# An mLSTM cell feeding a GELU MLP: the first chunk's order on TensorE, and split matmuls in the fifth chunk

## The chip, the cores and the metric

The kernel runs on one core of a Trainium2 chip. The metric is the device time of one execution in microseconds (us). Each time shown is that of one run; the median of the runs stands for the kernel. A profiled execution, with a trace of every instruction, comes beside them.

## The reference, cut to what matters

The first block is an mLSTM cell over 4 batches, 8 heads, 768 steps and a head size of 40; the second is a two-layer MLP on its output, laid out as 3072 tokens of 320 features.

```python
for t in range(S):                                   # S = 768
    m_new = np.maximum(f_gate[:, :, t] + m, i_gate[:, :, t])
    f_stab = np.exp(f_gate[:, :, t] + m - m_new)
    i_stab = np.exp(i_gate[:, :, t] - m_new)
    C = f_stab * C + i_stab * einsum('bhd,bhe->bhde', v_t, k_t)
    n = f_stab * n + i_stab * k_t
    h_tilde = einsum('bhde,bhe->bhd', C, q_t)
    denom = np.maximum(np.abs(einsum('bhd,bhd->bh', n, q_t)), 1.0)
    y[:, :, t] = sigmoid(o_gate[:, :, t]) * h_tilde / denom
x = y.transpose(0, 2, 1, 3).reshape(3072, 320)
h = x @ w_in                                         # 320 x 2048
g = h * sigmoid(1.702 * h)
out = g @ w_out                                      # 2048 x 320
```

All inputs and the output are float32.

## The kernel before, in words

Time is cut into six chunks of 128 steps, `w` = 0 to 5. Within a chunk the cell is computed like attention: scores of keys and queries, multiplied by exponents of gates, times values; a state is carried from chunk to chunk. Each chunk then gives 512 tokens (4 batches of 128) to the MLP: `up` or `up_fast` over 8 pairs `j` of 128 hidden features, then `down` or `down_fast`. Chunks 1 to 5 use Strassen-like forms (`up_fast`, `down_fast`), and the attention of chunk `w + 1` is threaded between the blocks of `down` of chunk `w`. There is no scheduler: every engine executes its instructions in the order in which the Python code issues them, and waits on semaphores where data or a buffer is not ready.

The first chunk, before any MLP work exists, stands alone at the start (lines 767 to 788). For each batch `b` it runs `transposes(0, b)` (keys and queries through TensorE into p_t, L347, copied by ScalarE), `scores(0, b - 1)` (p_s, L397, and on VectorE the multiplication L399 into `wt`), `weights(0, b)` (bf16 matmuls into p_w, L372 to L378, and exponents on ScalarE, L380). After the loop come `columns(0)` (L325, L327, L328), then for each batch `open_first` (a tanh of the output gate on ScalarE, L765) and `values` (L440, 8 matmuls with 41 moving columns each, two records per matmul in the trace; then `outputs` on VectorE, L418 to L427, and a copy on POOL, L431). Batch 0's values stand in the last turn of the loop, ahead of `scores(0, 3)`. Then four `seam` calls turn y into the MLP's layout: three TensorE transposes into p_x (L480) and a ScalarE copy into xT (L482). `up(0, j)` (L557, L563) needs all four.

`keep_busy(n, bank)` issues n bf16 matmuls of a tile of zeros; their results are not read. In the kernel before, the last seam has one ahead of its transposes and two behind, into the second bank of p_x.

MLP weights arrive as 512-column pieces of raw 32-bit words and are changed in place by `convert(n)`: two ScalarE operations (L229, L230), then four on VectorE (L231 to L236). Pieces 0 and 1 are converted within the first loop; piece 2 (`w_in_x`, the 64-row rest of w_in, read at L563) between the last two seams; the others during the up- and down-projections of chunk 0 (`weights_in`).

All DMAs of the start are issued by SyncE in one order: gates, keys and queries per batch with pieces 0 and 1 between, then v and o gates per batch, then pieces 2 to 9.

PSUM has two pools: `ps_a` (p_t, p_w, p_cols, p_x and others; a ring of two tiles of two banks) and `ps_m` (p_s, p_o, p_h, p_out; a ring of four tiles of one bank).

In `up_fast`, `rest()` (L629 to L632) multiplies the last 64 of the 320 features: two matmuls of 64 rows each, 512 columns, in the upper and lower half of the array, for the rows `row0` and `row1`. For even `j` it ends the accumulation, for odd `j` it begins it, so that two calls stand next to each other.

Of the kernel before, what the change touches and what calls it, by code (L numbers as in the profile page):

```python
# [8 lines left out]
FP = mybir.dt.float32  # L9
U32 = mybir.dt.uint32  # L10
# [7 lines left out]
L = 128  # L18
# [8 lines left out]
def kernel(  # L27
# [13 lines left out]
    B, H, S, D = q.shape  # L41
# [3 lines left out]
    NW = S // L  # L45
# [4 lines left out]
    W = B * L  # L50
# [16 lines left out]
    ps_m = ctx.enter_context(tc.tile_pool(name="ps_m", bufs=4, space=PSUM))  # L67
    ctx.enter_context(tc.manual_schedule())

    V, A, G, T = nc.vector, nc.scalar, nc.gpsimd, nc.tensor  # L70
# [15 lines left out]
    w_in_x = const.tile([128, NF // 2, 128], FP, name="w_in_x")  # L86
# [62 lines left out]
    pieces = []  # L149
# [4 lines left out]
    bits = {}  # L154
# [31 lines left out]
    def keep_busy(n, bank):  # L186
        for _ in range(n):
            T.matmul(bank, idle, idle.unsqueeze(1).to_broadcast([128, 4, 128]), start=True, stop=True)

    p_idle = ps_m.tile([128, W], FP, tag="m", name="p_idle")  # L190
# [31 lines left out]
    kT, qT, ys, xT, gs, o_ps, sums, vw, x_row = {}, {}, {}, {}, {}, {}, {}, {}, {}  # L222


    def convert(n):

        lo, hi, dst = bits[n][:, :, 0], bits[n][:, :, 1], pieces[n][0]
        dst_u = dst.bitcast(U32)
        A.activation(out=dst, in_=hi.bitcast(FP), func=AF.Abs)  # L229
        A.activation(out=lo, in_=lo, func=AF.Copy, scale=2.0 ** -29)  # L230
        V.tensor_scalar(out=dst, in0=dst, scalar1=HI_MIN, scalar2=HI_MAX, op0=OP.max, op1=OP.min)  # L231
        V.tensor_scalar(out=dst_u, in0=dst_u, scalar1=3, scalar2=0x3FFFFFFF, op0=OP.logical_shift_left,
                        op1=OP.bitwise_and)
        V.scalar_tensor_tensor(out=dst_u, in0=hi, scalar=0xC0000000, in1=dst_u, op0=OP.bitwise_and,
                               op1=OP.bitwise_or)
        V.tensor_tensor(out=dst_u, in0=dst_u, in1=lo, op=OP.add)  # L236
# [59 lines left out]
    def slot(i, x):  # L296

        return slice((x ^ i) * HL, (x ^ i) * HL + HL)

    def banks(name):  # L300
        return ps_a.tile([128, 2, 512], FP, tag="a", name=name)
# [131 lines left out]
    def values(w, c):  # L433
        if w == 0:
            hs = slice(c * H, (c + 1) * H)
            po = ps_m.tile([L, H, D1], FP, tag="m", name="p_o")
            for p in range(NP):
                for i in range(2):
                    h = 2 * p + i
                    T.matmul(po[:, h, :], wt[w, c][:, p, i, :], v_st[:, c * H + h, :], start=True, stop=True)  # L440
            outputs(w, hs, po)
            return
        hs = slice(c * PH, (c + 1) * PH)
        po, pi = banks("p_o"), banks("p_i")

        for j in range(NJ):
            for i in range(2):
                for x in range(2):
                    t, r = slice(x * HL, x * HL + HL), slot(i, x)
                    T.matmul(po[t, i, j * D1:(j + 1) * D1], wt[w, c][r, j, i, :], v_st[r, c * PH + 2 * j + i, :],  # L450
                             start=True, stop=True)
        for j in range(NJ):
            b, p = 2 * c + j // NP, j % NP
            for i in range(2):
                r = slice(i * 64, i * 64 + D)
                for x, s in enumerate((state[w % 2], state_mid)):
                    t = slice(x * HL, x * HL + HL)
                    T.matmul(pi[t, i, j * D1:(j + 1) * D1], qT[w, b][r, p, t], s[r, c * NJ + j, :], start=True,  # L458
                             stop=True)
        u = work.tile([L, PH, D1], FP, tag="u", name="u")  # L460
        v = u.rearrange("s (j i) d -> s i j d", i=2)
        g = cols[w][:, BH + c * PH:BH + (c + 1) * PH].rearrange("s (j i) -> s i j", i=2).unsqueeze(3)
        view = lambda z: z[:, :, 0:NJ * D1].rearrange("s i (j d) -> s i j d", d=D1)
        V.tensor_tensor(out=v, in0=view(pi), in1=g.to_broadcast([L, 2, NJ, D1]), op=OP.mult)
        V.tensor_tensor(out=v, in0=view(po), in1=v, op=OP.add)
        outputs(w, hs, u)
# [3 lines left out]
            xT[w] = work.tile([128, 3, B, L], FP, tag="xT", bufs=1, name="xT")  # L470
        return xT[w]

    def seam(w, c, b, busy=0, after=0):
        both = banks("p_x")
        px = both[:, 0, 0:3 * L]
        keep_busy(busy, both[:, 1, :])
        y = ys[w, c][:, b, :]
        for x in range(3):
            y_x = y[:, 256:384] if x == 2 else y[:, x:256:2]
            T.transpose(px[:, x * L:(x + 1) * L], y_x, ident)  # L480
        keep_busy(after, both[:, 1, :])
        A.copy(out=x_of(w)[:, :, 2 * c + b, :], in_=px.rearrange("r (x t) -> r x t", t=L))  # L482

    def x_square(c, n):
# [125 lines left out]
    def up_fast(w, j):  # L610

        x, rest_x = temps[w], xT[w].rearrange("p c b t -> p c (b t)")
        late = j % 2 == 0
        p1, row0 = (ps_m.tile([128, W], FP, tag="m", name="p_h") for _ in range(2))
        both = banks("p_h")
        row1 = both[:, 0, :]
        flat = both.rearrange("p i t -> p (i t)")  # L620
        left, right = slice(0, half_w), slice(half_w, W)
        f = lambda c, i: w_in_sb[:, c, (2 * j + i) * 128:(2 * j + i + 1) * 128]

        def product(n, out, start, stop):
            a = {1: lambda: f(0, 0), 2: lambda: f(1, 0), 3: lambda: s_in[:, 2, j], 4: lambda: f(1, 1),
                 5: lambda: s_in[:, 0, j], 6: lambda: s_in[:, 1, j], 7: lambda: f(0, 1)}[n]()
            T.matmul(out, a, x[n], start=start, stop=stop)  # L627

        def rest():  # L629
            for i, row in enumerate((row0, row1)):  # L630
                r = slice(i * 64, i * 64 + 64)
                T.matmul(row, w_in_x[r, j, :], rest_x[r, 2, :], start=not late, stop=late)  # L632

        def row_0():
            product(2, row0[:, left], late, False)
            product(3, row0[:, right], False, not late)

        def row_1():
            product(4, row1[:, left], late, False)
            product(7, row1[:, right], False, not late)  # L640

        if not late:
            rest()
        product(1, p1[:, left], True, True)
        if late:
            row_0()
        product(5, both[:, 1, left], True, True)
        product(6, both[:, 1, right], True, True)
        row_1()
        if late:  # L650
            rest()
        else:
            row_0()
        y = work.tile([L, 2, DM + 64], FP, tag="y", name="parts").rearrange("p a b -> p (a b)")
        u2 = second[w]
        g = gs[w, j] = gp.tile([128, 2, W], FP, tag="g", name="g")
        A.copy(out=y[:, left], in_=p1[:, left])  # L657
        if j:
            gelu_fast(w, j - 1)
        V.tensor_tensor(out=u2, in0=both[:, 1, right], in1=y[:, left], op=OP.add)  # L660
        V.tensor_tensor(out=y[:, half_w:3 * half_w].rearrange("p (a t) -> p a t", a=2),  # L661
                        in0=flat[:, half_w:3 * half_w].rearrange("p (a t) -> p a t", a=2),
                        in1=u2.unsqueeze(1).to_broadcast([128, 2, half_w]), op=OP.add)
        V.tensor_tensor(out=g[:, 1, :], in0=row1, in1=y[:, half_w:3 * half_w], op=OP.add)  # L664
        u = y.rearrange("p (a t) -> p a t", t=half_w)[:, 0:3:2]
        g0 = g[:, 0, :].rearrange("p (a t) -> p a t", a=2)
        if j < NF // 2 - 2:
            A.copy(out=g[:, 0, :], in_=row0)  # L668
            G.tensor_tensor(out=g0, in0=g0, in1=u, op=OP.add)  # L669
        else:  # L670
            V.tensor_tensor(out=g0, in0=row0.rearrange("p (a t) -> p a t", a=2), in1=u, op=OP.add)
# [91 lines left out]
    def open_first(b):  # L763
        hs = slice(b * H, (b + 1) * H)
        A.activation(out=eo[0][:, hs, :], in_=eo[0][:, hs, :], func=AF.Tanh, scale=0.5)  # L765

    for b in range(B + 1):
        if b < B:
            transposes(0, b)
        if b == B:  # L770
            open_first(0)
            values(0, 0)
        if b:
            scores(0, b - 1)
        if b in (1, 2):
            convert(b - 1)
        if b < B:
            weights(0, b)
    load_gates(1)
    load(1, "kq")  # L780
    columns(0)
    for b in range(1, B):
        open_first(b)
        values(0, b)
    for b, (busy, after) in enumerate(((0, 0), (0, 0), (0, 0), (1, 2))):
        seam(0, b // 2, b % 2, busy, after)
        if b == 2:
            convert(2)

    beside = [((3, 4), (10, 11, 12, 13, 14)), ((5, 6, 7), (15,)), ((8, 9, 10), (16,)), ((11, 12, 13), (17, 18, 19)),  # L790
              ((14,), ()), ((15,), ()), ((16,), ()), ((17,), ()), ((18,), ()), ((19,), ())]
# [112 lines left out]
```

## Time and profile before

| what | us |
|---|---|
| median of 3 runs | 479.73 |
| the runs | 479.73, 481.18, 478.07 |
| the profiled execution | 478.76 |
| its span, first to last instruction | 477.1 |

| engine | busy us | share of the span |
|---|---|---|
| PE (matmul) | 470.1 | 99% |
| PEld (weight load, overlaps PE) | 379.2 | 79% |
| DVE | 341.0 | 71% |
| ACT | 189.4 | 40% |
| POOL | 157.8 | 33% |

In the profile's lines "PE L440 MATMUL p_o<-v_st,wt" is TensorE, line 440 of the kernel, the output's tile and the tiles read. The page cuts the span into 40 slices of 11.9 us; its row PEclk gives the TensorE clock granted, in tenths. In a timeline a line has the start, the duration, the engine, the line, the operation, shapes and count, and in brackets the idle time before it and who ended it. In the chain of waits a line has the start, the time spent, and on what.

### The profile page before, as it was taken

What the parts mean: (1) busy time and instruction counts of PE and PEld (TensorE: products, weight loads), DVE (VectorE), ACT (ScalarE), POOL (GpSimd) and SP (SyncE); (2) the same over time, 40 slices, a digit from 0 to 9 for tenths busy, and PEclk for the clock granted to TensorE, in tenths of its full rate; (3) what the DMA queues carried; (4) which work ended last, traced back from release to release, by engine and by line L of the source; (5) the groups of instructions that cost most, each with busy time, mean ns of one, the idle gap of its engine ahead of it and who ended that gap; (6) DMA issues with size and microseconds to landing.
All of it is one profiled execution on the core that took longest, in us unless ns stands there. A gap on an engine that the chain in (4) does not pass through costs nothing.

```text
span 477.1 us, 12024 instructions
## 1 busy us (share of the span) xinstructions
PE 470.1 (99%) x4884; PEld 379.2 (79%) x4884; DVE 341.0 (71%) x701; ACT 189.4 (40%) x429; POOL 157.8 (33%) x145
## 2 busy tenths in 40 slices
PE   8999999999999999999999999999999999999997
PEld 5874446777767999767999877999877999876997
DVE  6755977989968877868877868887867866644612
ACT  4646567900434810354820254720254720164200
POOL 6020002500299720157620157620157620047100
PEclk9969999999999999999999999999999999999999
DMA  7999988005999105999205899305899205100000
GB/s 178 177 319 171 261 119 210 4 3 137 207 169 138 20 18 136 164 184 139 33 18 136 157 184 136 44 19 136 150 173 147 48 19 127 37 0 1 0 30 27
DMA packets 157591, 52.18 MB, mean 109 GB/s; under 512 B 127296, under 2 KB 154976, under 8 KB 157536
## 3 DMA queue, kind: packets, MB, share of 16 engines
q1 hardware_dynamic: 149536, 49.78, 56.4%
q10 hardware_dynamic: 8000, 1.64, 1.7%
q8 instruction: 38, 0.62, 0.6%
q14 instruction: 17, 0.14, 0.1%
HBM read 43.86 MB, written 7.54 MB: 108 GB/s over the span
## 4 chain that ended last, share of the span: by engine, by line
PE 95%; DVE 2%; DMA 1%; issue 1%; ACT 1%; SPq 0%; DVEq 0%
PE p_out L732 32%; PE p_h L627 26%; PE p_h L632 8%; PE p_out L678 7%; PE p_h L557 6%; PE p_c L535 3%; PE p_o L450 2%; PE p_o L440 2%; PE p_s L408 2%; PE p_i L458 2%; PE p_h L563 2%; PE p_t L347 1%; PE p_s L397 1%; DMA q_sq<-in_q_dram 1%; PE p_x L480 0%
## 5 line engine op out<-in xcount | busy, mean ns | idle before, releaser
L669 POOL TENSOR_TENSOR g<-g,parts 128x512 f32<-128x512 f32 x30 | 38.2, 1274 | 190.3 <-DVE parts L661 183.0
L657 ACT COPY parts<-p_h 128x256 f32<-128x256 f32 x40 | 15.0, 374 | 151.8 <-PE p_h L627 123.5
L732 PE MATMUL p_out<-w_out_sb,g 128*128 128x160 f32 x480 | 69.6, 301 | 0.2 <-ACT g L608 0.2
L732 PEld LDWEIGHTS p_out<-w_out_sb,g 128*128 128x128 f32 x480 | 66.5, 190 | 1.3 <-ACT g L608 0.5
L627 PE MATMUL p_h<-xT,w_in_sb 128*128 128x256 f32 x240 | 66.9, 388 | 0.0
L608 ACT ACTIVATE g<-g 128x512 f32<-128x512 f32 x80 | 50.1, 631 | 40.4 <-DVE g L664 25.8
L627 PEld LDWEIGHTS p_h<-xT,w_in_sb 128*128 128x128 f32 x240 | 43.7, 190 | 20.2 <-issue 7.6
L737 DVE TENSOR_TENSOR o_sb<-o_sb,p_out 128x160 f32<-128x160 f32 x70 | 21.5, 318 | 41.4 <-PE p_out L732 40.8
L732 PE MATMUL p_out<-t_sb,s 128*128 128x160 f32 x320 | 47.1, 300 | 0.0
L660 DVE TENSOR_TENSOR t_x<-p_h,parts 128x256 f32<-128x256 f32 x40 | 16.8, 421 | 39.3 <-PE p_h L632 34.9
L732 PEld LDWEIGHTS p_out<-t_sb,s 128*128 128x128 f32 x320 | 44.4, 190 | 0.2
L627 PE MATMUL p_h<-t_x,s_in 128*128 128x256 f32 x160 | 41.1, 379 | 0.0
L632 PE MATMUL p_h<-xT,w_in_x 64*128 64x512 f32 x160 | 39.7, 615 | 0.0
L384 ACT ACTIVATE wt<-wt,cols 128x64 f32<-128x64 f32 x160 | 38.8, 333 | 0.1
L525 POOL TENSOR_TENSOR vw<-v_st,cols 128x656 f32<-128x656 f32 x12 | 16.5, 1393 | 61.5 <-ACT cols L331 61.5
L678 PE MATMUL p_out<-w_out_sb,g 128*128 128x320 f32 x128 | 36.0, 436 | 0.7 <-DVE w_out_sb L236 0.7
L627 PEld LDWEIGHTS p_h<-t_x,s_in 128*128 128x128 f32 x160 | 30.3, 190 | 4.2
L678 PEld LDWEIGHTS p_out<-w_out_sb,g 128*128 128x128 f32 x128 | 23.8, 190 | 10.6 <-DVE w_out_sb L236 1.2
L557 PE MATMUL p_h<-xT,w_in_sb 128*128 128x512 f32 x64 | 29.5, 604 | 0.8 <-ACT xT L482 0.8
L661 DVE TENSOR_TENSOR parts<-p_h,t_x 128x512 f32<-128x512 f32 x40 | 27.7, 692 | 3.5
L668 ACT COPY g<-p_h 128x512 f32<-128x512 f32 x30 | 17.4, 581 | 29.3 <-PE p_h L632 24.4
L664 DVE TENSOR_TENSOR g<-p_h,parts 128x512 f32<-128x512 f32 x40 | 27.7, 692 | 1.4
(186 smaller groups left out, 839.0 us busy)
## 6 DMA issues: line engine op xcount, KB each, us to landing
wt<-m_row SPq DMA_DIRECT2D x40, 128.0 KB, 3.9
k_sq<-in_k_dram SPq DMA_DIRECT2D x16, 320.0 KB, 6.1
q_sq<-in_q_dram SPq DMA_DIRECT2D x16, 320.0 KB, 10.0
out_dram<-o_sb SPq DMA_DIRECT2D x24, 160.0 KB, 2.3
eo<-in_o_gate_dram SPq DMA_DIRECT2D x5, 640.0 KB, 9.1
bits<-in_moe_w_in_dram SPq DMA_DIRECT2D x6, 512.0 KB, 8.2
q_sq<-x_row SPq DMA_DIRECT2D x10, 256.0 KB, 2.9
v_st<-in_v_dram SPq DMA_DIRECT2D x14, 160.0 KB, 5.1
```

Source lines behind the costliest of these rows:

```text
L384: A.activation(out=x[:, h, :], in_=x[:, h, :], func=AF.Exp, scale=-1.0, bias=cols[w][:, c * PH + h:c * PH + h + 1])
L557: T.matmul(ph[j][i], w_in_sb[:, c, f * 128:(f + 1) * 128], x[:, c, :], start=(first and c == 0), stop=(not first and c == 1))
L608: A.activation(out=gs[w, j][:, i, :], in_=gs[w, j][:, i, :], func=AF.Gelu_apprx_sigmoid)
L627: T.matmul(out, a, x[n], start=start, stop=stop)
L632: T.matmul(row, w_in_x[r, j, :], rest_x[r, 2, :], start=not late, stop=late)
L661: V.tensor_tensor(out=y[:, half_w:3 * half_w].rearrange("p (a t) -> p a t", a=2), in0=flat[:, half_w:3 * half_w].rearrange("p (a t) -> p a ...
L664: V.tensor_tensor(out=g[:, 1, :], in0=row1, in1=y[:, half_w:3 * half_w], op=OP.add)
L668: A.copy(out=g[:, 0, :], in_=row0)
L669: G.tensor_tensor(out=g0, in0=g0, in1=u, op=OP.add)
L678: T.matmul(po, gs[w, f // 2][:, f % 2, b * L:(b + 1) * L], w_out_sb[:, f, :], start=(f == 0), stop=(f == NF - 1))
L732: T.matmul(po, a(f), b[:, f, :], start=(f == 0), stop=(f == NH - 1))
L737: V.tensor_tensor(out=dst, in0=x, in1=po, op=OP.add)
```

## The change

It has three parts.

In the first chunk, `values(0, 0)` moves ahead of `weights(0, 3)`, and `values(0, 1)` ahead of `scores(0, 3)`, each with its `open_first`; the other two stand between the seams. `convert(2)` is parted: its ScalarE half stands after seam 0, its VectorE half after the last seam.

`keep_busy` now writes to a tile of its own, `spare`, from the ring `ps_m`, and nine of its matmuls stand behind the seams (2, 2, 3, 2) in place of three.

In `up_fast`, at `w == NW - 2` (the fifth chunk) alone, `rest()` issues its matmuls in halves of 256 columns.

```diff
     def convert(n):
-
-        lo, hi, dst = bits[n][:, :, 0], bits[n][:, :, 1], pieces[n][0]
-        dst_u = dst.bitcast(U32)
+        convert_begin(n)
+        convert_end(n)
+
+    def convert_begin(n):
+        lo, hi, dst = words(n)
         A.activation(out=dst, in_=hi.bitcast(FP), func=AF.Abs)
         A.activation(out=lo, in_=lo, func=AF.Copy, scale=2.0 ** -29)
+
+    def convert_end(n):
+        lo, hi, dst = words(n)
+        dst_u = dst.bitcast(U32)
         V.tensor_scalar(out=dst, in0=dst, scalar1=HI_MIN, scalar2=HI_MAX, op0=OP.max, op1=OP.min)
...
-    def seam(w, c, b, busy=0, after=0):
-        both = banks("p_x")
-        px = both[:, 0, 0:3 * L]
-        keep_busy(busy, both[:, 1, :])
+    def seam(w, c, b):
+        px = banks("p_x")[:, 0, 0:3 * L]
...
-        keep_busy(after, both[:, 1, :])
...
         def rest():
-            for i, row in enumerate((row0, row1)):
-                r = slice(i * 64, i * 64 + 64)
-                T.matmul(row, w_in_x[r, j, :], rest_x[r, 2, :], start=not late, stop=late)
+            n = 2 if w == NW - 2 else 1
+            for h in range(n):
+                t = slice(h * W // n, (h + 1) * W // n)
+                for i, row in enumerate((row0, row1)):
+                    r = slice(i * 64, i * 64 + 64)
+                    T.matmul(row[:, t], w_in_x[r, j, :], rest_x[r, 2, t], start=(not late and h == 0),
+                             stop=(late and h == n - 1))
...
         if b == B:
-            open_first(0)
-            values(0, 0)
+            open_first(1)
+            values(0, 1)
         if b:
             scores(0, b - 1)
         if b in (1, 2):
             convert(b - 1)
+        if b == B - 1:
+            open_first(0)
+            values(0, 0)
         if b < B:
             weights(0, b)
     load_gates(1)
     load(1, "kq")
     columns(0)
-    for b in range(1, B):
-        open_first(b)
-        values(0, b)
-    for b, (busy, after) in enumerate(((0, 0), (0, 0), (0, 0), (1, 2))):
-        seam(0, b // 2, b % 2, busy, after)
-        if b == 2:
-            convert(2)
+    spare = ps_m.tile([128, W], FP, tag="m", name="p_idle")
+    seam(0, 0, 0)
+    keep_busy(2, spare)
+    convert_begin(2)
+    open_first(2)
+    values(0, 2)
+    seam(0, 0, 1)
+    keep_busy(2, spare)
+    open_first(3)
+    values(0, 3)
+    seam(0, 1, 0)
+    keep_busy(3, spare)
+    seam(0, 1, 1)
+    keep_busy(2, spare)
+    convert_end(2)
```

More of the change, by code (lines that the diff above doesn't have):

```diff
@@ L222, with words @@
     kT, qT, ys, xT, gs, o_ps, sums, vw, x_row = {}, {}, {}, {}, {}, {}, {}, {}, {}
+    def words(n):
+        return bits[n][:, :, 0], bits[n][:, :, 1], pieces[n][0]
     def convert(n):
-        lo, hi, dst = bits[n][:, :, 0], bits[n][:, :, 1], pieces[n][0]
-        dst_u = dst.bitcast(U32)
+        convert_begin(n)
+        convert_end(n)
+    def convert_begin(n):
+        lo, hi, dst = words(n)
         A.activation(out=dst, in_=hi.bitcast(FP), func=AF.Abs)
         A.activation(out=lo, in_=lo, func=AF.Copy, scale=2.0 ** -29)
+    def convert_end(n):
+        lo, hi, dst = words(n)
+        dst_u = dst.bitcast(U32)
         V.tensor_scalar(out=dst, in0=dst, scalar1=HI_MIN, scalar2=HI_MAX, op0=OP.max, op1=OP.min)
```

## The prediction

> **What bounds the kernel now.** I read the page first, then TensorE's waits over the whole span, then the windows around the one dip of the clock, and last the timelines of that stretch. Matmul covers 99% of the span, so only what delays TensorE counts. The clock row of the page, and TensorE's list of waits (us in total, times, longest):
>
> ```profile
> PEclk9969999999999999999999999999999999999999
> ```
>
> ```profile
> PE p_h L557 <- ACT xT L482: 0.8, 1, 0.8
> PE p_out L678 <- DVE w_out_sb L236: 0.7, 1, 0.7
> PE p_i L458 <- issue: 0.6, 1, 0.6
> ```
>
> Idle time is 3 us in all. The loss sits elsewhere: the third digit of the clock row is 6. Windows of 3.41 us (columns: PE busy, weight loads, DVE, ACT, POOL, granted clock, DMA share, GB/s) place it:
>
> ```profile
> 15.68:19.10 3.42, 3.42 (x39) 2.92 (x38) 2.71 (x5) 2.08 (x5) 0.00 (x0) 1.00 0.86 128
> 19.10:22.51 3.41, 3.41 (x38) 3.24 (x38) 2.40 (x7) 0.64 (x2) 0.24 (x1) 1.00 0.95 183
> 22.51:25.92 3.41, 3.41 (x18) 3.41 (x18) 1.66 (x7) 1.41 (x4) 0.24 (x1) 0.50 1.05 271
> 25.92:29.34 3.42, 3.42 (x18) 3.42 (x18) 1.38 (x5) 0.00 (x0) 0.23 (x1) 0.50 1.02 408
> 29.34:32.75 3.41, 3.41 (x16) 2.81 (x16) 1.38 (x5) 1.27 (x3) 0.94 (x2) 0.50 1.14 248
> 32.75:36.16 3.41, 2.57 (x10) 1.22 (x9) 2.44 (x3) 3.41 (x8) 1.79 (x2) 1.00 1.12 301
> ```
>
> Half clock lasts from 22.51 to 32.75, three windows, although PE is busy throughout. The timeline of TensorE says with what:
>
> ```profile
> 18.10 1.88 PE L440 MATMUL p_o<-v_st,wt 128*128 128x41 f32 x16
> 19.90 1.16 PE L397 MATMUL p_s<-qT,kT 40*128 40x128 f32 x16
> 21.14 9.10 PE L440 MATMUL p_o<-v_st,wt 128*128 128x41 f32 x48
> 30.03 2.37 PE L480 MATMUL p_x<-ident,y 128*128 128x128 f32 x9
> 34.45 3.70 PE L557 MATMUL p_h<-xT,w_in_sb 128*128 128x512 f32 x8 [0.84 <-ACT xT L482]
> ```
>
> Four batches of values stream 41 columns per weight load. Three of them in a row, and nine transposes, run cold. The up-projection starts at 34.45. A second, separate loss is late, in the chain of waits:
>
> ```profile
> 393.55 0.82 PE p_i L458 x54
> 394.37 0.62 issue
> ```
>
> TensorE stops 0.62 us inside a run of values with no semaphore to wait for.
>
> [...] 22.51 to 32.75 is 10.24 = 3 x 3.413. [...] here the window 29.34 to 32.75, mostly transposes, brought the clock back, so I count them. [...] the page shows 38 packets, 0.62 MB on TensorE's instruction queue[...].
>
> **First chunk, step by step.** I lay the new order on the durations of before: a values batch 1.71 (18.26 to 19.97 in the chain), scores 1.09, weights 1.43, columns 0.23, a warm transpose 0.11 (L347: eight in 0.88), a bf16 product of 512 columns 0.22. All engines keep their other order, and SP's order is unchanged.
>
> TensorE: scores(2) ends at 16.84; values(0) needs v_st of batch 0 (issued 10.23, landing 4.6 to 5.0 later), there by 15.3: to 18.55. Weights(3) to 19.98, values(1) to 21.69, scores(3) to 22.78, columns to 23.01, seam 0 to 23.34, two products to 23.8, values(2) to 25.5, seam 1 and two products to 26.25, values(3) to 27.96. No bank holds it up: the added tile shifts the ring of four by one, and what it reuses has been read.
>
> DVE: outputs(0) 18.6 to 20.1, outputs(1) 21.7 to 23.2 (1.48 each), the product with scores(3) to 24.5, columns copy 24.65. outputs(0) and (1) now stand before that product, which waits for nobody else but values(3).
>
> ACT: tanh of batch 0 goes ahead of the last exponents; its gate is issued at 12.21 and lands 3.9 to 5.5 later, by 17.7 at worst, and the exponents wait for weights(3) at 19.98 anyway: no cost. Exponents to 21.1, columns 24.85, xT 0 at 25.3. Now the first half of convert(2) stands here: its bits are issued 20.84 and land 5.3 later, 26.1. ACT stalls 0.8, converts to 27.4, and queued behind it are tanh(2), to 27.85, xT 1 and tanh(3), to 28.7. So outputs(2) waits: its multiply runs 27.85 to 28.3, y to 28.75, POOL's copy 0.24 to 29.0. Seam 2 ends 29.1 instead of 28.3: a new stall of 0.8. Three products to 29.75; outputs(3) to 30.25, POOL 30.5, seam 3 ends 30.6, its copy 0.45. The up-projection starts near 31.1. The last two products end by then: no cost. Of the nine products, six more than before, only the four of seams 0 and 1 (0.9) lie on the path, and half of that is hidden by the wait for y. Gain: 34.45 - 31.1 = 3.35, if the clock stays full. Before, the same conversion stood ahead of the last xT copy (32.81 to 34.04); that delay goes.
>
> convert_end(2) starts at 30.25 on DVE. The same four operations took 33.52 to 36.85 beside POOL's vw (the first one 1.31 instead of 0.42), so to 33.6; the first reader, the up-projection's rest, is at 31.1 + 3.63 = 34.7. Hidden, by 1.1. If that cover went, each us late costs one.
>
> Does the start of the up-projection carry to the end? DMA is near 1.0 until 58 us, so I looked at what is fed late: the fourth wt<-m_row is issued 71.14, lands near 75.0, read at 81.60, then 78.2; raw lands near 71.6, read 77.92, then 74.5; t_sb's last half near 79.7, read 86.56, then 83.2. Slack of 3 everywhere: the shift passes.
>
> **Does the clock stay?** I weigh streaming time by the share of rows and columns used: values 0.55 us of 1.71, scores 0.53 of 1.09, weights 1.07 of 1.43, transposes and products all. Before, the window that lost the clock (19.10 to 22.51) has 0.36, the one before it, which kept it, 0.57, and the lowest later one that kept it 0.52. The limit is between 0.36 and 0.52. After, on the same edges: 0.44, 0.47, 0.53, 0.45. Just inside the unknown span. A window of half clock costs up to 1.7, in the last one about 1 because there are waits; with another phase a window holding seam 1's products, values(3) and the wait falls to 0.38. I take no dip as likeliest, and keep 0 to 2.1 for the range.
>
> **Fifth chunk's rest.** Eight 64x512 matmuls become sixteen of 64x256 at w = 4, two row groups beside each other. Four junctions of 8 records take 1.92 each (340.82 to 342.74), 0.240 per record[...]. [...] 1.76 to 2.14 per junction, -0.6 to +0.9 in all. I take +0.1.
>
> What it also does is move instructions: in the program's order, with four instructions to an fp32 matmul and two to a transpose, TensorE's grow from 9893 to 9967, 10 in the first chunk and 64 here. The stall of 0.62 came at instruction 8900, 1.45 after a block landed (393.55). Blocks were fetched at 384.65, 388.18, 392.62: about 4 apart, and their borders were passed at 388.17, 391.23, 394.37: 3.1 apart, too fast. 74 later, the same borders fall at the work of 385.4, 389.5, 393.6: 4.1 apart. I take the stall as gone, -0.6; bounds -0.6 and +0.6 (another appears). The other chunks move by 10, in the same bursts: nothing.
>
> **Sum.** The profiled execution took 478.76 (span 477.1 and 1.66 around it). 478.76 - 3.35 - 0.6 + 0.1 = 474.9. It lies 0.97 below the median of the runs shown, 479.73 (478.07 to 481.18); window phase alone can make such differences in a stretch like this, so I carry half of it: 475.4.
>
> **Rivals.** (a) As above, 475.4, own range 474.3 to 476.4: 0.52. (b) One or two windows still fall to half clock, +1 to +2.1: 477.0; for it the densities 0.44 and 0.45, against it the seams spread among the values: 0.25. (c) More comes out: the bits land before ACT asks (0.7 back) and the halved matmuls gain 0.6: 474.1; against it the full DMA queues: 0.10. (d) Off the path: the clock stays, but the rest or w_out conversions end late and hand 2.5 back: 478; against it the slacks above: 0.08. (e) Slower: the window 15.68 to 19.10, thinned from 0.57 to 0.44 by moving values(0) into it, loses the clock at 19.10 and no later window regains it before the up-projection. 10.6 us of work are left then, doubled 21.2: start at 40.3, 5.85 late, 484.6 with the other terms. By my measure the first cold window would hold the rest of weights(3) and values(1), 0.54 at half clock, and bring the clock back; it decides from where that is not enough: 0.05.
>
> A measurement tells about 1% from no change, 474.9 to 484.5. Faster: all of (c) and under half of (a), 0.33. Slower: (e), 0.05. Range: (a) to (c) and (d)'s middle, 473.8 to 478.2.
>
> **What would show it.** Right: full clock in all windows between 5.4 and the end, p_h L557 from about 31.1, PE waiting near 28 and 30 for y, no issue wait near 390. Wrong: 0.50 in any window before 33; p_h later than 32.5; DVE's L236 of w_in_x holding L563; junctions of rest above 2.1.

## Result and profile after

The changed kernel takes 475.49 us, median of 5 runs (475.27 to 475.93), against 479.54 (478.07 to 481.18) for the kernel before, measured beside it: ratio 0.9918, 95% interval 0.9893 to 0.9943. So it is faster, by some 0.8% (0.6% to 1.1%). Its profiled execution took 475.49 with a span of 473.8, against 478.76 and 477.1.

The page's span and clock row, and three of TensorE's waits over the whole span (us in total, times, longest):

```profile
span 473.8 us, 12097 instructions
PEclk9999999999999999999999999999999999999999
```

```profile
PE p_s L417 <- DVE state L550: 0.8, 2, 0.5
PE p_x L487 <- DVE den L427: 0.5, 1, 0.5
PE p_x L487 <- DVE y L436: 0.2, 1, 0.2
```

The 6 in the clock row is gone. So are the wait of p_i for "issue" and the wait of p_h for ScalarE's copy. The wait of p_out for w_out_sb, 0.7, is there as before. New are two short waits of the seams (p_x) and, outside the part of the kernel that was reordered, 0.8 us in which the second chunk's scores (p_s) wait for VectorE. (L417 is the L408 of before; lines have moved by 6 to 10.)

The windows of 3.41 us again (columns as before; the clock is the number behind the five engines, here 1.00). The step of 3.41 is what the traces show: the granted clock was 0.50 for 10.24 in before (22.51 to 32.75) and for 3.41 in one_product (27.33 to 30.74), and in before it fell again at 476.48, 130 such steps behind 32.75. The edges here are laid back in steps of 3.413 from this execution's own fall to 0.50 near its end, at 472.94:

```profile
15.55:18.96 3.41, 3.41 (x39) 3.06 (x38) 2.99 (x6) 1.76 (x4) 0.00 (x0) 1.00 0.76 121
18.96:22.38 3.42, 3.42 (x39) 3.11 (x38) 1.73 (x8) 1.44 (x3) 0.24 (x1) 1.00 1.07 180
22.38:25.79 3.41, 3.41 (x35) 3.13 (x32) 2.32 (x7) 0.59 (x2) 0.24 (x1) 1.00 1.11 263
25.79:29.20 3.41, 2.90 (x24) 2.62 (x23) 1.99 (x9) 2.33 (x5) 0.24 (x1) 1.00 1.04 410
29.20:32.62 3.42, 3.12 (x12) 1.34 (x10) 3.28 (x6) 2.35 (x5) 2.66 (x3) 1.00 1.12 248
```

Full clock in all of them, though PE is less busy than before: 2.90 in the fourth, where before it was 3.42 at half clock. TensorE's timeline, and the ends of the two waits:

```profile
26.27 1.88 PE L449 MATMUL p_o<-v_st,wt 128*128 128x41 f32 x16
28.65 0.58 PE L487 MATMUL p_x<-ident,y 128*128 128x128 f32 x3 [0.51 <-DVE den L427]
30.04 0.67 PE L487 MATMUL p_x<-ident,y 128*128 128x128 f32 x3 [0.16 <-DVE y L436]
31.28 3.70 PE L563 MATMUL p_h<-xT,w_in_sb 128*128 128x512 f32 x8
```

The up-projection starts at 31.28 instead of 34.45. By the lead I mean how much earlier in its span the changed kernel runs a matmul than the kernel before runs the same one. It is 3.17 at the first up-projection, 2.05 behind the second chunk's scores, 2.34 ahead of the sixth chunk's last values, 3.26 behind them, and 3.27 at the end. So the first chunk won 3.17, 1.12 was given back in the second, 0.29 came in on the way, and 0.92 at the late stop. The chain of waits there shows the p_i run whole:

```profile
391.21 0.93 PE p_i L467 x64
392.15 1.96 PE p_out L742 x13
```

### The profile page after: what moved, and what is told of

The parts are those of the page before. It is cut to its first block, busy times and chain, and to the rows that moved or that the text cites. A ratio compares the mean times of both kernels' runs of the same rounds, so it can differ in the third digit from the quotient of the medians.

```text
span 473.8 us, 12097 instructions
## 1 busy us (share of the span) xinstructions
PE 466.7 (99%) x4922; PEld 378.7 (80%) x4922; DVE 342.9 (72%) x701; ACT 189.3 (40%) x429; POOL 158.7 (33%) x145
## 4 chain that ended last, share of the span: by engine, by line
PE 87%; SPq 4%; ACT 3%; DVE 2%; issue 1%; DMA 1%; DVEq 0%; ACTq 0%
PE p_out L742 33%; PE p_h L633 26%; PE p_h L641 8%; PE p_h L563 6%; PE p_out L688 3%; SPq L121 3%; PE p_o L459 2%; PE p_c L541 2%; PE p_i L467 2%; PE p_s L417 2%; PE p_h L569 2%; ACT wt L393 2%; DMA s_in<-in_moe_w_in_dram 1%; SPq L166 1%; PE p_t L356 1%
## 5 line engine op out<-in xcount | busy, mean ns | idle before, releaser
L641 PE MATMUL p_h<-xT,w_in_x 64*128 64x512 f32 (+1 forms) x192 | 39.8, 540 | 0.0
```

The source lines that it names most:

```text
L641: T.matmul(row[:, t], w_in_x[r, j, :], rest_x[r, 2, t], start=(not late and h == 0), stop=(late and h == n - 1))
```

## Experiments

Each kernel below was run beside the kernel before, on the same chip; the ratios are against that. The changed kernel itself was not run again, so a difference from its 475.49 is one between sessions, and less certain than a ratio or than what two traces show. Where I speak of density, it is the prediction's estimate: streaming time per window of 3.41 us, weighted by the share of rows and columns used. The streaming is worked out from paces in the traces: four float32 records of 256 columns in 0.87 in before (L627, 337.70 to 338.57), two bf16 products of 512 columns in 0.43 in the changed kernel (L188, 25.84 to 26.27). That the clock follows streaming weighted in this way is an assumption of mine; no run isolates it. A junction is two neighbouring calls of rest(), and a border is the place in TensorE's program where I take one block of instructions to end and the next to begin, 256 apart like the stops of no_products below.

**no_split: the changed kernel, rest() undivided.**

```diff
-            n = 2 if w == NW - 2 else 1
+            n = 1
```

> The changed kernel with rest() undivided in the fifth chunk, so that TensorE's instructions of the sixth chunk's attention stand 64 earlier, 10 from where they stood before the change. Theory: the split is worth its place in the instruction stream alone; undivided, a stop that waits for nothing (issue) of 0.4 to 0.7 us comes back in the second p_i run near 391, that run takes 1.9 instead of 1.05, and the junctions of rest take 1.92 instead of 1.93: 476.4 (0.9 more than 475.5). Rival: the 0.9 us gained there has another cause (the stores or the row transfers beside it): no stop, 475.5. First chunk as in the changed kernel under both: up-projection from 31.3.

476.32 us (475.88 to 478.27), ratio 0.9965 (0.9943 to 0.9987). The stop is back, in the chain of waits:

```profile
391.41 0.74 PE p_i L467 x49
392.15 0.52 issue
392.67 0.44 PE p_i L467 x15
```

The lead over the kernel before at the end is 2.30 instead of 3.27; the junctions of rest take 1.92. So 0.97 of the changed kernel's gain hangs on the split, although the split itself makes no work shorter. The instruction at which TensorE stops is again number 8900 of its program, as in the kernel before. The theory holds.

**split_only: the kernel before with the halved rest() alone** (the part of the change in `up_fast`).

> The kernel before the change with the halved rest() of the fifth chunk alone. Theory: nothing changes in the first chunk (half clock for about three windows), the stop near 395 is gone and the second p_i run takes 1.05 instead of 1.97; junctions 1.93 instead of 1.92. Time 478.6, 0.9 below before, within the spread that the clock's windows make. Rival: the stop stays, 479.5.

478.88 us in one run. No wait for issue is left in the trace; half clock lasts four windows here, 21.77 to 35.42, so that the up-projection starts 1.02 later than in the profiled execution of before, and the end is only 0.12 later: 0.90 came in at the stop. The junctions took 1.93, against 1.92 undivided. The two runs together price the split: +0.04 for its own work in four junctions, and 0.9 gained by the place of what follows.

**no_products: the changed kernel without the nine products of zeros.**

```diff
     seam(0, 0, 0)
-    keep_busy(2, spare)
     convert_begin(2)
...
```

> The changed kernel without any of the nine products of zeros; the order of values and seams stays. Theory: the clock is held by weighted streaming per window of 3.41 us, with the limit between 0.36 and 0.42; the window near 25.8 to 29.2 falls to about 0.25, so half clock follows from about 29.2 to 32.6, the up-projection starts near 31.2 but cold for 1.4 us: 476.3, 0.8 above 475.5. Rival: spreading the values is enough and the products are idle weight: clock full throughout, 475.4 or less (0.4 us of products come off the path between the seams, but the gate's tanh is awaited anyway).

480.15 us (479.01 to 482.47), ratio 1.0053 (1.0022 to 1.0083): slower than before. The clock falls, as the density said, behind this window. It does so at 28.12, some 1.1 us earlier than expected, and for two windows instead of one:

```profile
24.71:28.12 3.41, 2.55 (x23) 2.43 (x22) 1.44 (x6) 2.77 (x7) 0.00 (x0) 1.00 1.00 368
```

The density of this window is 0.27; in the next two the granted clock is 0.50. The up-projection starts at 31.20, hardly earlier than with the products, since the seams now wait longer; its first matmuls run at half clock, and by the first state product (p_c) the lead over before is down from 3.26 to 1.41. That accounts for 1.85, not for a kernel slower than before. The rest was not expected at all. The chain of waits in the second chunk's attention:

```profile
95.47 1.15 PE p_s L417 x60
96.62 1.06 issue
97.69 0.33 PE p_s L417 x4
...
104.27 0.75 issue
...
109.50 0.58 issue
```

Three stops without a wait, 2.4 us together. Counted in the program's order, they stand at instructions 1476, 1732 and 1988, 256 apart; the one of before stood at 8900. All four leave the remainder 196 when divided by 256. The instruction queue of the page (q8) had 38 packets in before, with 9893 instructions of TensorE, and 39 in the changed kernel, with 9967: some 260 to a packet. So I take the stops as borders of instruction blocks, one packet each; this is a reading. Without the products the border 1220 stands 4 instructions ahead of the second chunk's scores, which wait here for their bank; the next block was fetched at 95.12, after the scores had first been let go at 94.00. In the changed kernel the border stands 22 ahead, and the fetch came at 85.77, long before its scores started at 92.23.

**no_products_padded: the same, with nine tiny matmuls behind the last seam.**

```diff
+    for _ in range(9):
+        T.matmul(spare[:, 0:64], idle, idle[:, 0:64], start=True, stop=True)
     convert_end(2)
```

> The changed kernel without the nine products, but with nine matmuls of 64 columns of zeros behind the last seam, so that TensorE's later instructions stand exactly where they stand in the changed kernel. Theory: without them three stops that wait for nothing (1.07, 0.75, 0.58 us) came into the second chunk's attention since each block's border fell behind the scores' wait for their bank; with the places restored these stops vanish, and what stays is half clock for about two windows near the seams, 1.8 us: 477.4 (up-projection from 31.5, first matmuls cold). Rival: the stops come with the later start or with the cold clock and stay: 480.

477.32 us (476.68 to 479.26), ratio 0.9968 (0.9949 to 0.9986). The clock falls as before, from 28.24 for two windows; the fetch came at 87.62, and the three stops are gone. Its waits behind the start are these and two more of 0.5 to 0.7, none of them for "issue":

```profile
PE p_x L487 <- DVE den L427: 0.9, 1, 0.9
PE p_s L417 <- DVE state L550: 0.8, 2, 0.5
```

The theory holds: the nine products are worth some 1.8 us for the clock (477.32 against 475.49) and, by where they push the later code, another 2.8 (480.15 against 477.32).

**products_only: the order of before, two products behind each batch of values.**

```diff
             values(0, 0)
+            keep_busy(2, ps_m.tile([128, W], FP, tag="m", name="p_idle"))
...
         values(0, b)
+        keep_busy(2, ps_m.tile([128, W], FP, tag="m", name="p_idle"))
```

> The kernel before the change with one edit: two products of zeros, in a tile of their own, behind each of the four batches of values; order and rest() as before. Theory of the density: windows of about 0.45 and 0.42 hold the clock or fall just short of it; if they hold it, the up-projection starts near 31.3 like in the changed kernel, the instruction stop of the sixth chunk stays or wanders with 8 added instructions, 476.4. If it falls once, half clock for one or two windows, start 32 to 33, 477 to 478. Rival: the order itself is what counts (values apart from each other): half clock near 22.5 for three windows as before and more work in it, 480 or more.

476.21 us (475.90 to 476.91, 20 runs), ratio 0.9955 (0.9941 to 0.9969). The clock holds in all 20 runs (their mean granted clock is 0.999 or 1.000), and in the trace it does so with the first of these windows at a density of 0.40:

```profile
21.42:24.84 3.42, 3.42 (x32) 3.28 (x31) 2.69 (x9) 1.41 (x4) 0.24 (x1) 1.00 1.12 219
24.84:28.25 3.41, 3.41 (x30) 3.13 (x30) 1.92 (x9) 0.00 (x0) 0.47 (x2) 1.00 1.00 379
```

So the clock needs the products and not the new order. The up-projection starts at 31.72, 0.44 later than in the changed kernel, after a wait of 1.1 for ScalarE's copy, which stands behind both ScalarE operations of the conversion of piece 2. The stop of the sixth chunk is there with 0.40. The lead over before grows from 2.74 at the up-projection to 2.87 at the end: nothing is given back in the second chunk.

**one_product: the same with one product.**

> As products_only (order and rest() of before), but with one product of zeros behind each batch of values instead of two. Theory of the density: one 0.213 us product in each 1.92 us lifts a run of values from 0.32 to about 0.40, with the scores' window near 0.41; kept windows so far went down to 0.40, a lost one had 0.36, so in part of the runs the clock falls for one or two windows: 476.0 where it holds, 477 to 478 where not, and the runs spread by over 1 us. Rival: [...] all runs near 475.8 with full clock, or all near 478.6 as before.

475.58 us, ratio 0.9923 (0.9899 to 0.9948), but the runs spread from 474.95 to 478.02. In the profiled execution, of 476.14 us, the clock falls for one window, behind one of density 0.36:

```profile
23.91:27.33 3.42, 3.42 (x33) 3.40 (x33) 2.53 (x9) 0.57 (x2) 0.45 (x2) 1.00 1.00 335
27.33:30.74 3.41, 3.41 (x16) 2.62 (x16) 1.38 (x5) 1.63 (x4) 1.71 (x4) 0.50 1.05 345
```

As the theory said, this is at the edge: the mean granted clock on record is full in six of the twelve runs, down by one window (0.996) in four and by two (0.992) in two. The sixth chunk's stop is there too, with 0.35. Where the clock holds, one product less per batch is even the better bargain (474.95 against 475.90 for the best runs).

**tanh_first: the changed kernel, both tanhs ahead of convert(2)'s ScalarE half.**

```diff
-    convert_begin(2)
     open_first(2)
...
     open_first(3)
+    convert_begin(2)
     values(0, 3)
```

> The changed kernel with the ScalarE half of convert(2) moved behind the tanhs of batches 2 and 3 instead of ahead of both. Theory: outputs(2) waited 1.25 us for the tanh queued behind the conversion, which itself waited for its bits; now the multiply runs at 26.25, y 2 is ready near 27.2, seam 2 follows values(3) at 28.0 without a wait, outputs(3) ends 29.5, and the up-projection starts near 30.5 instead of 31.28: 474.7. Rival: the copies of xT or convert_end take the place of the wait (the conversion still ends near 27.2, its VectorE half the earlier the later): start 31.2, 475.5.

474.55 us (fourteen of fifteen runs 474.44 to 474.83), ratio 0.9919 (0.9898 to 0.9939). The time is as expected, the reason is not. Seam 2 waits no longer, but seam 3 does:

```profile
27.94 0.57 PE L487 MATMUL p_x<-ident,y 128*128 128x128 f32 x3
29.79 0.67 PE L487 MATMUL p_x<-ident,y 128*128 128x128 f32 x3 [0.62 <-DVE y L436]
```

The up-projection starts at 31.02, earlier by 0.26 and not by 0.8: behind the first wait stood another, values(3), its outputs and POOL's copy. The other 0.7 is what was not lost in the second chunk, where the scores didn't wait in this trace. The fifteenth run took 478.29, with a mean clock of 0.996.

**carry_first: pieces 17 to 19 converted one block later.**

```diff
-            if w == 0 and i < 6:
-                weights_in(4 + i)
+            if w == 0 and i in (0, 1, 2, 4, 5, 6):
+                weights_in(4 + i - i // 4)
```

> The changed kernel with the conversions of pieces 17, 18 and 19 issued one block of the first down-projection later, so that the state additions of the first carry stand ahead of piece 17 on VectorE. Theory: the 0.83 us for which the scores of the second chunk wait for p_c's banks (and 1.1 us of shift lost there) come from piece 17's conversion, which stands ahead of the additions and met POOL's selects; gone, the kernel ends 0.8 to 1.1 earlier: 474.6. Rival: the additions are late for another reason (p_c's own products or the decays on POOL): no gain, 475.5; or the later pieces now hold up the down-projection: 476 or more.

474.63 us (474.12 to 475.71), ratio 0.9917 (0.9885 to 0.9949). To read it, first VectorE and POOL in the changed kernel, and behind them VectorE in the kernel before (L236 is the same line as L245):

```profile
88.69 1.50 DVE L245 CUSTOM_DVE_ANT_0 w_out_sb<-t_sb,w_out_sb 128x1024 uint16<-128x1024 uint16 x1 [0.52 <-ACT wt L393]
90.12 0.49 DVE L550 TENSOR_TENSOR state_mid<-p_c,state_mid 128x328 f32<-128x328 f32 x1
```

```profile
88.52 2.68 POOL L397 TENSOR_SCALAR_AFFINE_SELECT wt<-wt 64x1024 f32<-64x1024 f32 x2 [3.71 <-ACT wt L393]
```

```profile
91.50 0.69 DVE L236 CUSTOM_DVE_ANT_0 w_out_sb<-t_sb,w_out_sb 128x1024 uint16<-128x1024 uint16 x1
```

Piece 17's last operation takes 1.50 beside POOL's selects and starts 0.52 late. In the kernel before the same operation takes 0.69 and starts at 91.50, 0.19 ahead of the selects. The state additions (L550) behind it come 1.2 late, and they free the banks that the scores wait for. With the piece behind them the additions start here at 87.01:

```profile
87.01 0.49 DVE L550 TENSOR_TENSOR state_mid<-p_c,state_mid 128x328 f32<-128x328 f32 x1
```

No wait for p_s is left among TensorE's; the lead at the end exceeds that at the up-projection by 1.25, as against 0.10 in the changed kernel.

This fits the theory, but carry_first alone doesn't prove it: its up-projection started at 31.73, and products_only, which started at 31.72 with the pieces where they were, gave nothing back either. The profiles together say more. In four of them (the changed kernel, no_split, no_products, no_products_padded) piece 17's last operation took 1.45 to 1.51 and the scores waited 0.8. In the seven others that leave the piece ahead of the additions it took 0.69 and the scores didn't wait. So the 1.1 us went where this operation ran long. Why it came second to the selects there is not settled, since in all of these profiles the two stand some 0.2 us apart; and why it takes longer beside them no run isolates.

**products_early_convert: products_only, plus the split rest(), plus convert(2) parted, its ScalarE half ahead of the seams.**

```diff
+    convert_begin(2)
     for b, (busy, after) in enumerate(((0, 0), (0, 0), (0, 0), (1, 2))):
         seam(0, b // 2, b % 2, busy, after)
-        if b == 2:
-            convert(2)
+        if b == 3:
+            convert_end(2)
```

> Order of the kernel before, two products behind each batch of values (as in products_only), plus the halved rest() of the fifth chunk, plus convert(2) parted, its ScalarE half ahead of the seams, where ScalarE is idle, its VectorE half behind the last seam. Theory: full clock as in products_only; ScalarE's 1.07 us ahead of the last xT copy goes, the up-projection starts near 30.7 instead of 31.72; the stop of the sixth chunk goes: 474.3. Rival: the last y and its copy on POOL are late anyway, start 31.3, 475.2.

474.67 us (474.64 to 475.13), ratio 0.9915 (0.9875 to 0.9955): between theory and rival, for a third reason. In the profiled execution (475.13, the slowest of the seven) the last xT copy on ScalarE was released by the last of the idle products, not by its transposes:

```profile
31.09 0.48 ACT L491 COPY xT<-p_x 128x384 f32<-128x384 f32 x1 [0.50 <-PE p_x L188]
```

**early_convert_own_bank: the same, with the last seam's three products in a tile of their own.**

```diff
-    for b, (busy, after) in enumerate(((0, 0), (0, 0), (0, 0), (1, 2))):
+    for b, (busy, after) in enumerate(((0, 0), (0, 0), (0, 0), (0, 0))):
...
         if b == 3:
+            keep_busy(3, ps_m.tile([128, W], FP, tag="m", name="p_idle"))
             convert_end(2)
```

> As products_early_convert, but the last seam's three products go to a tile of their own behind its transposes. Theory: the last xT copy was released by the products (L188) in the second bank of its own tile p_x, 0.5 us after the transposes it needs; in a bank of their own they don't hold it: start of the up-projection 0.5 earlier after its third product's place is moved, 474.2 against 474.67. Rival: the copy was late for y and the path is the same: 474.7.

474.09 us (ten of twelve runs 474.00 to 474.31), ratio 0.9910 (0.9882 to 0.9938). The copy now waits for its transposes alone, and the up-projection follows the products at once:

```profile
29.05 1.00 PE L489 MATMUL p_x<-ident,y 128*128 128x128 f32 x6 [0.23 <-ACT xT L491]
29.89 0.81 PE L188 MATMUL p_idle<-t_sb 128*128 128x512 bf16 x3
30.62 2.41 PE L566 MATMUL p_h<-xT,w_in_sb 128*128 128x512 f32 x5
```

This is the best version: 1.4 below the changed kernel's median, without the new order of values and seams. It shows that the part of the change called "a tile of its own" has a value apart, up to 0.6 in this setting (474.67 to 474.09); the edit also moved one product from ahead of the last transposes to behind them, and no run parts the two. Two of the twelve runs took 475.88 and 476.19 at full clock, for a reason that is not known.

**tanh_and_carry: tanh_first and carry_first together.**

> Both orders: tanhs ahead of convert(2)'s ScalarE half (tanh_first), and pieces 17 to 19 one block later (carry_first). Theory: the first gives 0.25 at the start of the up-projection, where the last y (values(3), outputs(3), POOL) now bounds it; the second makes the second chunk's scores safe from the meeting of VectorE and POOL and keeps all of the shift: 474.2. Rival: in tanh_first that meeting went well already, so nothing is added: 474.55.

474.54 us (474.45 to 474.76), ratio 0.9896 (0.9845 to 0.9947). The rival was right: the meeting went well in tanh_first already, so there was nothing for the second edit to save.

## Why the prediction was right, and where it was not

The forecast of 475.4 met 475.49, but the sum behind it was 474.9 for the profiled execution, which took 475.49, and 0.48 was added for the runs' median. The sum missed by 0.6, and the allowance happened to cover that: the closeness of the forecast is luck.

**First chunk: right.** Start of the up-projection forecast 31.1, measured 31.28. The steps fall where they were laid: values(0) ends at 18.56 (18.55), the conversion waits 0.66 for its bits (0.8), outputs(2)'s multiply 27.49 (27.85), PE's two waits 0.51 and 0.16. VectorE's convert_end ended at 34.08 (33.6), still ahead of the rest at 34.91. The order of before in products_only loses only 0.44 of it.

**Clock: right, and now bounded.** The densities on this execution's edges are 0.42, 0.47, 0.53 and 0.43, against 0.44, 0.47, 0.53 and 0.45 forecast. A window of 0.40 kept the clock in products_only; windows of 0.36 lost it in before, split_only and one_product. By this measure, which is an estimate, the limit lies between the two.

For regaining the clock my measure fails. A window of 0.56 did not lift it in split_only and one of 0.65 not in no_products_padded, while 0.46 to 0.49 did at the start of several executions. The two failing windows hold transposes. Counting a transpose fully is too much; counting none is too little, since the window of before that lifted the clock, 29.34 to 32.75, would be left with about 0.2, and the one in no_products_padded that did not would keep 0.29. What weight would fit stays open.

Rival (b) did not show in the five runs of the changed kernel, but five are few. no_split, whose first chunk is the same, has a mean clock of 0.996 in three of twelve runs, which is one window lost, and these took 477.23 to 478.27. products_only has none in twenty. So the new order seems nearer the edge than the old one with products, although its thinnest profiled window is the denser one (0.43 against 0.40).

The products aren't free either. In the four of 97 later runs in which the kernel before lost one window alone (0.996), it took 475.00 to 475.61, no more than the changed kernel at full clock. As far as the mean clock tells, then, the new order and the products pay by holding the clock, and not by less work.

**The shift passes: wrong, by 1.12.** This is the step that failed: that the start's gain passes to the end because everything fed by DMA has slack. I compared the DMA-fed reads with the new times and found slack of 3, and left out VectorE's own order against POOL. There, the conversion of piece 17 stands ahead of the state additions that free the scores' banks; it ran 0.8 longer and 0.5 later, and the scores waited 0.8. The measured loss is 1.12 of 3.17. Rival (d) named the wrong holder and too high a price, but was the right kind.

**The stop: right in kind, size off.** Gone as forecast, worth 0.92 (0.97 by no_split), not 0.6. The wait of 0.62 was only its idle part: the ten matmuls behind it took 0.42, where the 64 of the run without a stop take 0.93. That it came from borders passed faster (3.1 apart) than blocks were fetched (4 apart) was my estimate; the runs show that it stands at instruction 8900 in before and in no_split, and is gone where the code stands 64 or 74 later (split_only, the changed kernel). The sentence "the other chunks move by 10: nothing" was right for the changed kernel and would have been badly wrong without the products, where three stops came in (no_products).

**The split: +0.04 instead of +0.1**, inside the bounds of 1.76 to 2.14 a junction, which were an estimate of mine that no run isolates. What the traces show: 16 records of 256 columns at 0.121 each take what 8 of 512 columns take at 0.240. (The prediction's "eight matmuls" are the eight records of one junction; there are 16 matmuls in all four, which become 32.)

**Not foreseen:** 0.29 on the way between the second chunk and the sixth, of which 0.24 is the wait of p_out for ACT's g at 158 that the changed kernel doesn't have. In sum, against the forecast: 0.18 less at the start and 1.12 given back; then more by 0.33 on the way (0.29 and the split's 0.04, counted apart), 0.06 at the split and 0.32 at the stop. That leaves 0.59.

## What to carry to other kernels

A stretch in which TensorE is busy all the time can still lose its clock (before: 3.41 of 3.41 busy from 19.10 to 22.51, then a granted 0.50): look at how much it streams per window, and where that is thin (here 0.36 lost the clock and 0.40 kept it, by my estimate), put a product of nothing between, in a PSUM tile that no other engine waits for. Use no more of them than hold the clock, and look at many runs: here one product per batch held it in six of twelve, two in all twenty. Before trusting that an earlier start reaches the end, list for each later stage what each engine's own queue has ahead of the operation that frees a bank, not the transfers alone. And when an edit adds or removes TensorE instructions, compare padded with unpadded: what follows may change by more than the edit (here 2.8 us, 480.15 against 477.32).

## What the runs showed of the hardware

- Stops without a wait stood at one remainder of the instruction count, 196 when divided by 256, in before (0.62), no_split (0.52), products_only (0.40), one_product (0.35) and no_products (1.06, 0.75, 0.58). At these stops TensorE went on 1.3 to 1.5 us after the block had landed (393.55 to 395.00 in before).
- In no_products, where scores wait just behind a border, the next block was fetched at 95.12, against 87.62 with the instructions in their old places (no_products_padded). That the wait held the fetch back is a reading of this one pair.
- The trace of before has one stop without a wait behind its start (0.62), against 38 packets on its instruction queue; no_products has three, in runs of small matmuls, of up to 1.06 us.
- The kernel before took 475.00 to 481.75 us in the 97 runs of the later sessions, in clusters near 475.3, 476.8, 478.4, 479.9 and 481.4. The mean granted clock recorded with each run orders them: 0.996, 0.993, 0.989, 0.986, 0.982. A window of 3.41 us at half clock takes 0.0036 off the mean of a span of 477, so these are one to five windows lost, at about 1.5 us each. The profiled executions agree: three windows at 0.989 (before) and four at 0.986 (split_only). The fall came at 22.51 in the one and at 21.77 in the other, whose first chunk is the same.
- In products_early_convert ScalarE's copy of one bank of a two-bank PSUM tile waited 0.5 us longer than for its transposes, until products written to the other bank were done.
